# Block-diagonal products on 64-row tiles of TensorE, one transposed Y for the features' transform, and a Nyquist row in two parts

## The chip, the cores and the metric

The kernel runs on one core of one Trainium2 chip. The metric is the device time of one execution in microseconds (us), lower is better; the number given for a kernel is the median of its runs. A core has TensorE (PE, matrix products; its weight loads are listed as PEld), VectorE (DVE), ScalarE (ACT), GpSimd (POOL) and SyncE (SP), which here issues the DMAs. Products write into PSUM, which has eight banks of 512 f32 columns on 128 partitions; DVE and ACT read it.

## What is computed

Three layers, batch 8, sequence 576, width 512 (8 heads of 64):

```python
# 1. Nystroem attention, m = 32 landmarks, per batch and head
A = sm(q, k_lm); Bm = sm(q_lm, k_lm); C = sm(q_lm, k)      # softmaxes
Z = ...                                                     # six steps Z = 2 Z - Z Bm Z
x = A @ Z @ C @ v
# 2. Fourier mixing and a feed-forward layer
u = x + real(fft(fft(x, axis=seq), axis=feature))
un = (u - mean(u)) / sqrt(var(u) + 1e-6)
y = u + relu(un @ w_ch1) @ w_ch2
# 3. gated channel mixing with a token shift
out = sigmoid(xr @ w_r) * (relu(xk @ w_k) ** 2 @ w_v)
```

## The kernel before

**Stages.** The attention and the mixing (`phase1`) work per batch; layer 2 (`norm`, `block_a`) works on nine blocks of 512 tokens, layer 3 (`prep`, `Gated`) on the same nine blocks behind it. Block i needs the batches that cover its tokens, so block 0 needs batch 0, and block 1 batches 0 and 1. While `block_a(i)` runs its long stream of f16 products (tiles `ph`, banks 4 and 5, and `acc`, banks 0 to 3), the products of later batches and normalisations are put between them. They take their PSUM tile, `gp`, from the banks left, and those are two once the blocks run; `psum(2)` takes two at once. Three blocks of `u` (tiles `ub`) fit in SBUF.

**Order.** Nothing is ordered by hand. `Plan.record` writes down each operation with its engine, an estimated cost and what it depends on; `Plan.issue` (line 375) then simulates the engines and gives each engine a fixed order: of the operations that are ready, the one with the longest tail of work behind it plus its stage's lead goes first (line 141: block products 1000, the start 400, batches 200, conversions of weights 170). DMAs stand in SyncE's queue in the same way. Where the simulation leaves PE idle, it puts in filler products (`warm`, line 1037: tile `spare`, or zeros added into the open `acc`). The products of the blocks are chained in their written order. The estimate of a product (`mm`, line 322) is its columns, four times for f32, divided by 4 or 2 where its weights have at most 32 or 64 columns, as such products lie beside each other on column tiles of the array. In the profile an f32 product has two records and an f32 transpose one.

**Weights.** `w_ch1` and `w_ch2` come as 64-bit numbers and are converted on ACT and DVE piece by piece (`Weights.run`: tiles `wst`, `wtop`, `more`, into `w1h`, `w1l`, `w2h`, `w2l`) while batch 0 and block 0 run.

**A batch.** `chain_a` makes the scores A (three tiles `A0` to `A2` of 97 rows, line 663), folds them by the sequence's symmetry, multiplies them with cosines and sines over the sequence (tiles `acs`: AC and AS) and transposes them (tile `at`: AT). `chain_b` and `series` (line 806) give Y = Z C v per head, four heads to a group g of 128 partitions (32 landmarks of each head). Line 817 writes it out as block diagonal `bdY`: 256 columns per group, where head h's 32 rows hold its 64 features and the other rows hold zeros (`mask4`).

**The tail of a batch** (line 894) is what the diff is about:
- `bdY` is transposed in four pieces, of which only the blocks on the diagonal are copied to `YT`.
- The features' transform: four products of `YT` pieces (128 rows, 64 columns) with `cs` (128 x 512 each) give cosine and sine parts `YC`, `YS` and the Nyquist column `yn`; two products side by side on two column halves of the array.
- `mixed(j)` (line 927) multiplies YC with AC and YS with AS for the 128 frequencies of slot block j, and DVE (or POOL) forms difference and sum, d1 and d2, in one buffer each.
- `xu(t)` (line 947) does x = A Y for slot block t = 0 to 3: two products with a piece of `bdY` as 128 x 128 weights, of 289 and 288 columns; DVE adds d and writes `u`.
- The Nyquist row is two products of one column of weights over 289 columns, which ACT copies into row 0 of d1 and d2 between `xu(0)` and `xu(2)`.

**norm(i)** (line 1111) has two forms. For i < 2 the mean is four products with `ones` on the four tiles of u, and the sum of squares 32 records of products of one column (`one`). For later blocks DVE and POOL add the four tiles first, the mean is one product, POOL adds the squares, and `token_sums` transposes them in four pieces, which DVE reduces.

Of the kernel before, what the change touches and what calls it, by code (L numbers as in the profile page):

```python
# [37 lines left out]
def slot_features():  # L38
    f = np.arange(DM)
    f[257:] = 512 - np.arange(1, 256)  # L40
    return f
# [151 lines left out]
class Plan:  # L193
# [127 lines left out]

    def mm(self, out, lhsT, rhs, start, stop, chain=False, **kw):

        cost = wide(rhs) / 2400.0 + 0.0025
        if rhs.dtype == F32:
            cost = max(4 * cost, 0.17)
        share = 4 if wide(lhsT) <= 32 else 2 if wide(lhsT) <= 64 else 1

        def run():
            self.nc.tensor.matmul(  # L330
                out.real(), lhsT=lhsT.real(), rhs=rhs.real(), start=start, stop=stop, **kw
            )

        op = self.record("pe", run, cost / share, [out], [lhsT, rhs])
# [244 lines left out]
def phase1(a, iss, psum, const, pool, ident, ublock):  # L579
# [162 lines left out]
    def chain_b(b):  # L742
# [63 lines left out]
        def series():  # L806
# [21 lines left out]
            g_.tensor_copy(bdY[:, 1, 0:1], bdY[:, 1, 256:257])  # L828

# [64 lines left out]
    def tail(b):  # L894

        bdY = T["bdY", b]
        psT = psum()[0]
        for pr in range(4):
            g, hp = pr // 2, pr % 2
            tr(  # L900
                psT[:, 128 * pr:128 * pr + 128],
                bdY[:, g, g + 128 * hp:g + 128 * hp + 128], ident,
            )
        YT = tile([128, 2, 2, 64], "YT", "t1")
        pT = psT.rearrange("p (g x) -> p g x", g=2)
        s_.activation(YT[:, :, 0], pT[:, :, 0:64], AF.Copy)
        s_.activation(YT[:, :, 1], pT[:, :, 192:256], AF.Copy)
        YC, YS = [
# [4 lines left out]
        g_.memset(YS[:, :, 0:1], 0.0)  # L913
        for g in range(2):
            ps = psum()[0]
            for hp in range(2):
                mm(
                    ps[64 * hp:64 * hp + 64, :], YT[:, g, hp, :], cs[:, 2 * g + hp, :],
                    True, True,
                )  # L920
            s_.activation(YC[:, g], ps[:, 0:256], AF.Copy)
# [5 lines left out]
        def mixed(j):  # L927
            pc, pq = psum(2)
# [7 lines left out]
            s_.activation(cp, pc[:, 0:HS], AF.Copy)  # L936
            d1 = tile([128, HS], "d1")
            d2 = tile([128, HS], "d2")
            v_.tensor_tensor(d1, cp, pq[:, 0:HS], op=ALU.subtract)
# [3 lines left out]
            else:  # L943
                v_.tensor_tensor(d2, cp, pq[:, 0:HS], op=ALU.add)
            return d1, d2

        def xu(t, da, db):
            g = t // 2
            pa, pb = psum()[0], psum()[0]
            lt = bdY[:, g, 128 * (t % 2):128 * (t % 2) + 128]  # L950
            mm(pa[:, 0:HS], lt, AT[0][:, g], True, True)
            mm(pb[:, 0:288], lt, AT[1][:, g, 0:288], True, True)
            base = S * b
            for i, lo, hi in cuts(base, base + HS):
                v_.tensor_tensor(
                    ublock(i)[t][:, lo - BLK * i:hi - BLK * i],
                    pa[:, lo - base:hi - base], da[:, lo - base:hi - base], op=ALU.add,
                )
            end = base + S
            for i, lo, hi in cuts(base + HS, end):  # L960
                l, h = lo - BLK * i, hi - BLK * i
                v_.tensor_tensor(
                    ublock(i)[t][:, h - 1:(l - 1 if l else None):-1],
                    pb[:, end - hi + 1:end - lo + 1], db[:, end - hi + 1:end - lo + 1],
                    op=ALU.add,
                )
# [12 lines left out]

# [11 lines left out]
def build(nc, tc, a):  # L991
# [5 lines left out]
    with stack, tc.manual_schedule():  # L997
# [113 lines left out]
        def norm(i):  # L1111
# [15 lines left out]
            if i < 2:  # L1127
                ps = gp()[0]
# [274 lines left out]
def consts():  # L1403
    mask2 = np.zeros((128, 2), np.float32)
    mask4 = np.zeros((128, 4), np.float32)
    for p in range(128):
        mask2[p, p // 64] = 1.0 / 18
        mask4[p, p // 32] = 1.0
    eye32 = np.tile(np.eye(M, dtype=np.float32), (4, 1))
    bones = np.kron(np.eye(4), np.ones((M, M))).astype(np.float32)  # L1410
# [13 lines left out]
    kk = np.arange(257)  # L1424
    for i in range(4):
        for p in range(128):
            f = 128 * i + p if i < 2 else 511 - (128 * (i - 2) + p)
            ang = 2 * np.pi * ((f * kk) % DM) / DM
            cs[p, i, 0:257] = np.cos(ang)
            cs[p, i, 257:512] = np.sin(ang[1:256])  # L1430
    return dict(
        mask2=mask2, mask4=mask4, eye32=eye32, bones=bones,
        ident=np.eye(128, dtype=np.float32),
# [48 lines left out]
```

## Time and profile before

| | us |
|---|---|
| median of 3 runs | 1536.48 (1536.45 to 1540.12) |
| the profiled execution | 1536.68 |
| its span, from the first to the last instruction | 1534.9 |
| PE busy in the span | 1522.2 |
| DVE, ACT, POOL busy in the span | 818.0, 578.2, 287.2 |

The profile lists every instruction of one execution with start and duration. Groups of instructions are named as out<-in by the program's tiles, with rows*columns of the weights and rows x columns of the moving operand for a product. Products are pipelined, so a product's duration holds its latency; how long it holds the engine is read from one start to the next. The timeline merges like instructions that follow each other; its columns are start, time from the first start to the last end, engine, line, operation, tiles, shape and count, and in brackets idle time before. PEclk is the granted share of TensorE's clock.

### The profile page before, as it was taken

To read this page: it belongs to the slowest core of one execution; us is meant where nothing else is said; L and a number is where in the kernel's file an instruction comes from. 1 tells how busy PE (TensorE), PEld (TensorE's weight loads), DVE (VectorE), ACT (ScalarE), POOL (GpSimd) and SP (SyncE) were. 2 spreads that over 40 slices of the span, in tenths; PEclk is the share of its full clock that TensorE was granted. 3 is DMA by queue.
4 is the path that set the end of the run, shared out by engine and by line. 5 is a ranking of instruction groups with operands and counts; after the bars stand their busy time and mean duration, and the time that the engine had idled before them with its cause. 6 is when DMAs were issued, how large, how long until landed. Compare 5 with 4: busy or idle time off the path is not lost.

```text
span 1534.9 us, 20950 instructions
## 1 busy us (share of the span) xinstructions
PE 1522.2 (99%) x8284; PEld 777.8 (51%) x8284; DVE 818.0 (53%) x1698; ACT 578.2 (38%) x1181; POOL 287.2 (19%) x351
## 2 busy tenths in 40 slices
PE   9999999999999999999999999999999999999998
PEld 5655555555645645645544444444444444444443
DVE  7888667667636426426135171212777765653222
ACT  4667464445413213213212131113655544443221
POOL 3021103113102102102002040001544432231100
PEclk9999999999999999999999999999999999999999
DMA  8434252433301001000004000002011101000000
GB/s 290 159 125 153 79 179 73 144 122 123 101 35 63 32 28 62 2 28 1 1 28 165 1 28 1 28 0 83 28 56 55 55 28 55 28 13 16 28 28 28
DMA packets 43586, 97.86 MB, mean 64 GB/s; under 512 B 4064, under 2 KB 9440, under 8 KB 42976
## 3 DMA queue, kind: packets, MB, share of 16 engines
q1 hardware_dynamic: 43488, 96.53, 18.4%
q8 instruction: 65, 1.06, 0.3%
q14 instruction: 33, 0.27, 0.1%
HBM read 72.39 MB, written 24.12 MB: 63 GB/s over the span
## 4 chain that ended last, share of the span: by engine, by line
PE 96%; DMA 1%; DVE 1%; ACT 1%; issue 0%; SPq 0%; POOL 0%; ACTq 0%; DVEq 0%
PE ph L330 37%; PE acc L330 36%; PE gp L330 21%; PE gp L346 2%; DMA ident<-in_ident 1%; DMA wst<-in_w_ch 0%; DVE small L186 0%; PE spare L1043 0%; SPq L315 0%; DVE uc L186 0%; DMA out<-o 0%; DVE d L186 0%; ACT d L186 0%; ACT wtop L186 0%; DVE o L186 0%
## 5 line engine op out<-in xcount | busy, mean ns | idle before, releaser
L330 PE MATMUL ph<-un,w1h 128*128 128x512 f16 x1152 | 349.9, 379 | 0.4 <-DVE uc L186 0.3
L330 PE MATMUL acc<-h,w2h 128*128 128x512 f16 x1152 | 348.5, 379 | 0.0
L186 DVE SCALAR_TENSOR_TENSOR h<-ph,h 128x512 f16<-128x512 f32 x144 | 99.2, 689 | 302.6 <-ACT h L186 302.2
L186 ACT ACTIVATE h<-ph 128x512 f16<-128x512 f32 x144 | 85.9, 596 | 390.7 <-PE ph L330 390.4
L330 PE MATMUL ph<-un,w1l 128*128 128x512 f16 x576 | 218.6, 380 | 0.0
L330 PE MATMUL acc<-h,w2l 128*128 128x512 f16 x576 | 218.3, 379 | 0.1
L330 PE MATMUL ph<-xk,w_k 128*128 128x512 f16 x864 | 199.6, 379 | 0.0
L330 PE MATMUL acc<-w_v,k 128*128 128x512 f16 x864 | 198.9, 379 | 0.0
L330 PEld LDWEIGHTS <-w2h 128*128 128x128 f16 x1152 | 113.0, 99 | 128.4 <-issue 5.7
L330 PEld LDWEIGHTS <-w1h 128*128 128x128 f16 x1152 | 112.7, 99 | 127.8 <-issue 7.4
L330 PEld LDWEIGHTS <-k 128*128 128x128 f16 x864 | 84.5, 98 | 100.6
L330 PEld LDWEIGHTS <-w_k 128*128 128x128 f16 x864 | 84.5, 98 | 99.7
L186 DVE TENSOR_TENSOR rk<-rk 128x512 f32<-128x512 f32 x72 | 55.5, 770 | 146.3 <-ACT rk L186 145.9
L330 PE MATMUL gp<-w_r,xr 128*128 128x512 f16 x432 | 99.3, 379 | 0.7 <-ACT rs L186 0.7
L186 ACT ACTIVATE rk<-ph 128x512 f32<-128x512 f32 x72 | 42.9, 596 | 129.2 <-PE ph L330 121.6
L330 PEld LDWEIGHTS <-w1l 128*128 128x128 f16 x576 | 57.1, 99 | 65.1 <-issue 4.4
L330 PEld LDWEIGHTS <-w2l 128*128 128x128 f16 x576 | 56.7, 98 | 63.2 <-issue 0.6
L186 DVE TENSOR_TENSOR k<-rk,k 128x512 f16<-128x512 f32 x72 | 59.3, 823 | 29.2 <-ACT k L186 29.0
L186 POOL TENSOR_TENSOR sq<-sq 128x513 f32<-128x513 f32 x27 | 36.7, 1360 | 198.6 <-ACT sq L186 198.1
L186 POOL TENSOR_TENSOR xr<-xt,xr 128x512 f16<-128x512 f32 x36 | 48.6, 1374 | 112.1 <-ACT xr L186 112.0
L330 PEld LDWEIGHTS <-xr 128*128 128x128 f16 x432 | 42.3, 98 | 51.4 <-issue 0.9
L186 DVE TENSOR_TENSOR xt<-xt,rs 128x512 f32<-128x512 f32 x72 | 60.5, 869 | 2.9 <-ACT rs L186 2.8
(162 smaller groups left out, 1919.1 us busy)
## 6 DMA issues: line engine op xcount, KB each, us to landing
wst<-in_w_ch SPq DMA_DIRECT2D x24, 512.0 KB, 3.9
q<-in_q SPq DMA_DIRECT2D x16, 578.0 KB, 5.1
k<-in_k SPq DMA_DIRECT2D x16, 576.0 KB, 4.9
ys<-ub SPq DMA_DIRECT2D x36, 256.0 KB, 2.1
out<-o SPq DMA_DIRECT2D x36, 256.0 KB, 2.1
yb<-ys SPq DMA_DIRECT2D x8, 1026.0 KB, 5.1
v<-in_v SPq DMA_DIRECT2D x8, 1024.0 KB, 5.9
more<-in_w_ch SPq DMA_DIRECT2D x8, 512.0 KB, 4.6
```

Source lines behind the costliest of these rows:

```text
L186: f(real(out), *map(real, args), **{k: real(x) for k, x in kw.items()})
L330: self.nc.tensor.matmul(out.real(), lhsT=lhsT.real(), rhs=rhs.real(), start=start, stop=stop, **kw)
L346: self.nc.tensor.transpose(out.real(), in_.real(), ident.real())
```

## The change

Per batch, on the same numbers:
- `bdY` gets two heads' columns instead of four (`maskp` in place of `mask4`): rows 0 to 63 and rows 64 to 127 now hold two heads each, in the same 128 columns. A dense `Y` is kept beside it.
- One transpose of `Y` (both groups beside each other) replaces the four of `bdY`. `cs` is laid out anew, so that each head is one product with 64 rows and 32 columns of weights; the eight of them stand on eight tiles of the array and write two banks.
- `xu(g)` does both slot blocks of a group: pairs of products, on rows 0 to 63 and rows 64 to 127, into two banks taken together; first the two of 289 columns, then the two of 288.
- Both `mixed` come first, with four tiles d1 to d4; d3 and d4 lie in the slots of A0 and A1.
- The Nyquist row is split at column 145 into two parts on two column tiles; ACT copies it in four pieces, and two rows are copied from d3 and d4 to d1 and d2, as the slots of two features change places.
- The planner's cost of a product is divided by 2 where two row tiles lie beside each other (`beside`).
- `norm(1)` takes the form of the later blocks.

```diff
 def slot_features():
     f = np.arange(DM)
-    f[257:] = 512 - np.arange(1, 256)
+    f[257:384] = 512 - np.arange(1, 128)
+    f[385:] = 384 - np.arange(1, 128)
+    f[256], f[384] = 384, 256
...
-        op = self.record("pe", run, cost / share, [out], [lhsT, rhs])
+        op = self.record("pe", run, cost / share / beside, [out], [lhsT, rhs])
...
+    maskp = load_const("maskp", [128, 2])
...
-        A = [tile([97, 2, 256], f"A{c}") for c in range(3)]
+        A = [
+            tile([128, 512], f"A{c}")[0:97].rearrange("p (x m) -> p x m", x=2) for c in range(3)
+        ]
...
-            bdY = T["bdY", b] = tile([128, 2, 260], "bdY")
+            bdY = T["bdY", b] = tile([128, 2, 130], "bdY")
+            Y = T["Y", b] = tile([128, 2, D], "Y")
...
+                s_.activation(Y[:, g], psY[:, D * g:D * g + D], AF.Copy, scale=rc[:, g:g + 1])
                 v_.scalar_tensor_tensor(
-                    bdY[:, g, g:g + 256].rearrange("p (h d) -> p h d", d=D),
-                    psY[:, D * g:D * g + D].unsqueeze(1).to_broadcast([128, 4, D]),
-                    rc[:, g:g + 1], mask4.unsqueeze(2).to_broadcast([128, 4, D]),
+                    bdY[:, g, g:g + 128].rearrange("p (h d) -> p h d", d=D),
+                    psY[:, D * g:D * g + D].unsqueeze(1).to_broadcast([128, 2, D]),
+                    rc[:, g:g + 1], maskp.unsqueeze(2).to_broadcast([128, 2, D]),
...
-        for pr in range(4):
-            g, hp = pr // 2, pr % 2
-            tr(
-                psT[:, 128 * pr:128 * pr + 128],
-                bdY[:, g, g + 128 * hp:g + 128 * hp + 128], ident,
-            )
-        YT = tile([128, 2, 2, 64], "YT", "t1")
...
+        tr(psT[:, 0:128], T["Y", b].rearrange("p g d -> p (g d)"), ident)
+        YT = tile([128, 2, 128], "YT", "t1")[:, 0]
+        s_.activation(YT, psT[:, 0:128], AF.Copy)
...
-        for g in range(2):
-            ps = psum()[0]
-            for hp in range(2):
+        ps2 = psum(2)
+        for h in range(4):
+            for g in range(2):
+                r = slice(64 * g, 64 * g + 64)
                 mm(
-                    ps[64 * hp:64 * hp + 64, :], YT[:, g, hp, :], cs[:, 2 * g + hp, :],
-                    True, True,
+                    ps2[g][M * h:M * h + M, :], YT[r, M * h:M * h + M], cs[r, h, :],
+                    True, True, beside=2, tile_position=(64 * g, M * h),
                 )
...
+        def xu(g, ds):
+
+            rows = [slice(64 * x, 64 * x + 64) for x in range(2)]
             base = S * b
+            end = base + S
+            pa = psum(2)
+            for x, r in enumerate(rows):
+                mm(pa[x][:, 0:HS], bdY[r, g, 0:128], AT[0][r, g], True, True, beside=2)
+            for x in range(2):
+                for i, lo, hi in cuts(base, base + HS):
+                    v_.tensor_tensor(
+                        ublock(i)[2 * g + x][:, lo - BLK * i:hi - BLK * i],
+                        pa[x][:, lo - base:hi - base], ds[x][0][:, lo - base:hi - base],
+                        op=ALU.add,
+                    )
+            pb = psum(2)
+            for x, r in enumerate(rows):
+                mm(pb[x][:, 0:288], bdY[r, g, 0:128], AT[1][r, g, 0:288], True, True, beside=2)
...
+        d1, d2 = tile([128, HS], "d1"), tile([128, HS], "d2")
+        d3, d4 = [tile([128, 512], n, t)[:, 0:HS] for n, t in (("d3", "A0"), ("d4", "A1"))]
+        mixed(0, d1, d2)
+        mixed(1, d3, d4)
+        xu(0, ((d1, d2), (d3, d4)))
+
+        s_.activation(d1[0:1, :], d3[0:1, :], AF.Copy)
+        s_.activation(d2[0:1, :], d4[0:1, :], AF.Copy)
+        psN = psum()[0]
+        parts = (0, 0, 145), (32, 145, HS)
+        for g in range(2):
+            for p, lo, hi in parts:
+                mm(
+                    psN[p:p + 1, lo:hi], yn[:, g:g + 1], AC[:, g, lo:hi], g == 0, g == 1,
+                    tile_position=(0, p),
                 )
...
-        d1, d2 = mixed(0)
-        xu(0, d1, d2)
-        psN = psum()[0]
-        for g in range(2):
-            mm(psN[0:1, 0:HS], yn[:, g:g + 1], AC[:, g], g == 0, g == 1)
-        s_.activation(d1[0:1, :], psN[0:1, 0:HS], AF.Copy)
-        s_.activation(d2[0:1, :], psN[0:1, 0:HS], AF.Copy)
-        xu(2, d2, d1)
-        d1, d2 = mixed(1)
-        xu(1, d1, d2)
-        xu(3, d2, d1)
+        for d in (d3, d4):
+            for p, lo, hi in parts:
+                s_.activation(d[0:1, lo:hi], psN[p:p + 1, lo:hi], AF.Copy)
+        xu(1, ((d2, d1), (d4, d3)))
...
-            if i < 2:
+            if i < 1:
```

The last edit stands twice, at lines 1116 and 1127.

## Rows read from the trace of the kernel before

**Rows 1.** The page, parts 1 and 4: busy time and the chain of waits.
```profile
PE 1522.2 (99%) x8284; PEld 777.8 (51%) x8284; DVE 818.0 (53%) x1698; ACT 578.2 (38%) x1181; POOL 287.2 (19%) x351
...
PE 96%; DMA 1%; DVE 1%; ACT 1%; issue 0%; SPq 0%; POOL 0%; ACTq 0%; DVEq 0%
```

**Rows 2.** Stretches start:end, length; busy us and count by engine; clock; DMA.
```profile
5.00:70.00 65.00, 62.49 (x472) 40.96 (x469) 55.10 (x139) 35.18 (x91) 12.50 (x17) 1.00 0.67 235
77.00:207.00 130.00, 129.27 (x833) 71.37 (x833) 100.91 (x236) 79.95 (x164) 23.80 (x30) 0.99 0.38 124
340.00:455.00 115.00, 115.00 (x688) 62.75 (x687) 67.61 (x161) 44.62 (x101) 17.51 (x21) 1.00 0.29 95
```
In rows 2 the engines stand in the order PE, PEld, DVE, ACT, POOL.

**Rows 3.** Groups of PE by tiles and shape, fillers: busy, mean ns, idle before.
```profile
L1043 PE MATMUL spare<-zero 128*128 128x512 f16 x89 | 24.5, 415 | 2.3 <-POOL zero L186 2.3
...
L1043 PE MATMUL acc<-zero 128*128 128x512 f16 x13 | 3.5, 380 | 0.0
```

**Rows 4.** Timeline of PE, batch 7: transposes and the features' transform.
```profile
737.43 0.60 PE L346 MATMUL gp<-ident,bdY 128*128 128x128 f32 x4
737.87 0.41 PE L346 MATMUL gp<-ident,A 96*128 96x96 f32 x3
...
738.55 0.38 PE L330 MATMUL acc<-h,w2h 128*128 128x512 f16 x1
738.86 1.95 PE L330 MATMUL gp<-c_cs,YT 128*64 128x512 f32 x8
740.74 0.39 PE L330 MATMUL acc<-h,w2h 128*128 128x512 f16 x1
```

**Rows 5.** Timeline of PE, batch 6: Nyquist row and a product with bdY.
```profile
689.30 0.59 PE L330 MATMUL ph<-un,w1h 128*128 128x512 f16 x2
689.83 1.14 PE L330 MATMUL gp<-acs,yn 128*1 128x289 f32 x4
690.89 0.39 PE L330 MATMUL ph<-un,w1l 128*128 128x512 f16 x1
691.12 0.65 PE L330 MATMUL gp<-at,bdY 128*128 128x289 f32 x2
691.61 0.59 PE L330 MATMUL acc<-h,w2h 128*128 128x512 f16 x2
```

**Rows 6.** Timeline of PE, normalisation of block 1: mean, then squares.
```profile
169.10 3.64 PE L330 MATMUL gp<-ub,one 128*128 128x512 f32 x8
172.58 0.38 PE L330 MATMUL acc<-h,w2l 128*128 128x512 f16 x1
...
175.39 3.63 PE L330 MATMUL gp<-one,tmp 128*128 128x1 f32 x32
178.88 0.61 PE L330 MATMUL ph<-un,w1h 128*128 128x512 f16 x2
```

**Rows 7.** The stretch behind it, in the columns of rows 2.
```profile
179.00:183.00 4.00, 4.00 (x16) 1.26 (x14) 3.32 (x15) 0.00 (x0) 0.91 (x2) 0.57 0.00 0
```

**Rows 8.** Timeline of PE at the start: batch 0's tail, block 0's mean and first product.
```profile
43.02 1.30 PE L330 MATMUL gp<-acs,Ae 128*128 128x289 f32 x4 [0.86 <-ACT Ae L186]
...
49.72 1.16 PE L330 MATMUL gp<-kbd,q 128*97 128x64 f32 x12
50.71 1.20 PE L330 MATMUL gp<-acs,Ae 128*128 128x289 f32 x4
...
61.09 3.67 PE L330 MATMUL gp<-ub,one 128*128 128x512 f32 x8
...
77.34 0.89 PE L330 MATMUL ph<-un,w1h 128*128 128x512 f16 x2 [0.26 <-DVE uc L186]
```

**Rows 9.** Timeline of SyncE's queue: the issue of a small constant.
```profile
6.69 0.33 SPq L315 DMA_DIRECT2D c_eye<-in_eye  x1
```

**Rows 10.** Timeline of DVE: the low half of the last piece of w_ch2.
```profile
202.65 0.68 DVE L186 SCALAR_TENSOR_TENSOR w2l<-wst,w2h 128x512 f16<-128x512 f32 x1
```

**Rows 11.** Timeline of PE: block 0's last products with that piece.
```profile
204.12 0.60 PE L330 MATMUL acc<-h,w2h 128*128 128x512 f16 x2
```

More of the change, by code (lines that the diff above doesn't have):

```diff
@@ L320, in load, with mm @@
         )
-    def mm(self, out, lhsT, rhs, start, stop, chain=False, **kw):
+    def mm(self, out, lhsT, rhs, start, stop, chain=False, beside=1, **kw):
         cost = wide(rhs) / 2400.0 + 0.0025
@@ L821, in series @@
             for g in range(2):
+                s_.activation(Y[:, g], psY[:, D * g:D * g + D], AF.Copy, scale=rc[:, g:g + 1])
                 v_.scalar_tensor_tensor(
-                    bdY[:, g, g:g + 256].rearrange("p (h d) -> p h d", d=D),
-                    psY[:, D * g:D * g + D].unsqueeze(1).to_broadcast([128, 4, D]),
-                    rc[:, g:g + 1], mask4.unsqueeze(2).to_broadcast([128, 4, D]),
+                    bdY[:, g, g:g + 128].rearrange("p (h d) -> p h d", d=D),
+                    psY[:, D * g:D * g + D].unsqueeze(1).to_broadcast([128, 2, D]),
+                    rc[:, g:g + 1], maskp.unsqueeze(2).to_broadcast([128, 2, D]),
                     op0=ALU.mult, op1=ALU.mult,
                 )
-            g_.tensor_copy(bdY[:, 1, 0:1], bdY[:, 1, 256:257])
+            g_.tensor_copy(bdY[:, 1, 0:1], bdY[:, 1, 128:129])
         return series
@@ L897, in tail @@
         psT = psum()[0]
-        for pr in range(4):
-            g, hp = pr // 2, pr % 2
-            tr(
-                psT[:, 128 * pr:128 * pr + 128],
-                bdY[:, g, g + 128 * hp:g + 128 * hp + 128], ident,
-            )
-        YT = tile([128, 2, 2, 64], "YT", "t1")
-        pT = psT.rearrange("p (g x) -> p g x", g=2)
-        s_.activation(YT[:, :, 0], pT[:, :, 0:64], AF.Copy)
-        s_.activation(YT[:, :, 1], pT[:, :, 192:256], AF.Copy)
+        tr(psT[:, 0:128], T["Y", b].rearrange("p g d -> p (g d)"), ident)
+        YT = tile([128, 2, 128], "YT", "t1")[:, 0]
+        s_.activation(YT, psT[:, 0:128], AF.Copy)
         YC, YS = [
@@ L913, in tail @@
         g_.memset(YS[:, :, 0:1], 0.0)
-        for g in range(2):
-            ps = psum()[0]
-            for hp in range(2):
-                mm(
-                    ps[64 * hp:64 * hp + 64, :], YT[:, g, hp, :], cs[:, 2 * g + hp, :],
-                    True, True,
+        ps2 = psum(2)
+        for h in range(4):
+            for g in range(2):
+                r = slice(64 * g, 64 * g + 64)
+                mm(
+                    ps2[g][M * h:M * h + M, :], YT[r, M * h:M * h + M], cs[r, h, :],
+                    True, True, beside=2, tile_position=(64 * g, M * h),
                 )
+        for g, ps in enumerate(ps2):
             s_.activation(YC[:, g], ps[:, 0:256], AF.Copy)
@@ L925, in tail, with mixed @@
         AT = T["at", b]
-        def mixed(j):
+        def mixed(j, d1, d2):
             pc, pq = psum(2)
@@ L936, in mixed @@
             s_.activation(cp, pc[:, 0:HS], AF.Copy)
-            d1 = tile([128, HS], "d1")
-            d2 = tile([128, HS], "d2")
             v_.tensor_tensor(d1, cp, pq[:, 0:HS], op=ALU.subtract)
@@ L944, in mixed @@
                 v_.tensor_tensor(d2, cp, pq[:, 0:HS], op=ALU.add)
[L945 to L952, printed above, removed]
-            base = S * b
[L954 to L957, printed above, removed]
-                )
[L959 to L966, printed above, removed]
@@ L968, in tail @@
-        d1, d2 = mixed(0)
-        xu(0, d1, d2)
-        psN = psum()[0]
-        for g in range(2):
-            mm(psN[0:1, 0:HS], yn[:, g:g + 1], AC[:, g], g == 0, g == 1)
-        s_.activation(d1[0:1, :], psN[0:1, 0:HS], AF.Copy)
-        s_.activation(d2[0:1, :], psN[0:1, 0:HS], AF.Copy)
-        xu(2, d2, d1)
-        d1, d2 = mixed(1)
-        xu(1, d1, d2)
-        xu(3, d2, d1)
+        def xu(g, ds):
+            rows = [slice(64 * x, 64 * x + 64) for x in range(2)]
+            base = S * b
+            end = base + S
[12 more added lines that the diff above has]
+                mm(pb[x][:, 0:288], bdY[r, g, 0:128], AT[1][r, g, 0:288], True, True, beside=2)
+            for x in range(2):
+                for i, lo, hi in cuts(base + HS, end):
+                    l, h = lo - BLK * i, hi - BLK * i
+                    v_.tensor_tensor(
+                        ublock(i)[2 * g + x][:, h - 1:(l - 1 if l else None):-1],
+                        pb[x][:, end - hi + 1:end - lo + 1],
+                        ds[x][1][:, end - hi + 1:end - lo + 1], op=ALU.add,
+                    )
@@ L1126, in norm @@
             r, t1, var = small(), small(), small()
-            if i < 2:
+            if i < 1:
                 ps = gp()[0]
@@ L1405, in consts @@
     mask4 = np.zeros((128, 4), np.float32)
+    maskp = np.zeros((128, 2), np.float32)
     for p in range(128):
@@ L1408, in consts @@
         mask4[p, p // 32] = 1.0
+        maskp[p, p // 32 % 2] = 1.0
     eye32 = np.tile(np.eye(M, dtype=np.float32), (4, 1))
@@ L1424, in consts @@
     kk = np.arange(257)
-    for i in range(4):
+    for h in range(4):
         for p in range(128):
-            f = 128 * i + p if i < 2 else 511 - (128 * (i - 2) + p)
+            f = D * h + p if p < D else 511 - D * h - (p - D)
             ang = 2 * np.pi * ((f * kk) % DM) / DM
-            cs[p, i, 0:257] = np.cos(ang)
-            cs[p, i, 257:512] = np.sin(ang[1:256])
+            cs[p, h, 0:257] = np.cos(ang)
+            cs[p, h, 257:512] = np.sin(ang[1:256])
     return dict(
-        mask2=mask2, mask4=mask4, eye32=eye32, bones=bones,
+        mask2=mask2, mask4=mask4, maskp=maskp, eye32=eye32, bones=bones,
         ident=np.eye(128, dtype=np.float32),
```

## The prediction

> **What bounds the kernel now.** I read the page's busy times and its chain of waits first: TensorE (PE) is busy for nearly the whole span, and the chain that ended last is 96% PE [rows 1]. A busy PE can still be one that only fills time, so the second look is at the filler products, which the planner puts where it expects PE to idle. 89 of them go to a spare bank and 13 to an open accumulator [rows 3]; the 13 add zeros in the stretch of block 0, and behind it there are none. So I cut the run in three. **Start**, up to 77 us: PE waits for batch 0's chain and for the normalisation of block 0, and fills. **Front**, 77 to 207 us, block 0: PE is full, but DVE (VectorE) is busy for 101 of 130 us and ACT (ScalarE) for 80, because the weights are converted here [rows 2]. **Rest**, from 207 us on: PE is full with DVE at 68 and ACT at 45 of 115 us [rows 2]. In the rest a microsecond taken from PE is a microsecond of time. Batches 2 to 7 lie there; batch 1 and the normalisation of block 1 lie in the front, batch 0 in the start.
>
> **The change, part by part, per batch.** I read a product's cost from one start to the next, not from its duration, which holds the pipeline's latency.
>
> Transposes: four start in 0.44 us (737.43 to 737.87) [rows 4]. One stays at 0.11, so -0.33.
>
> Products with cs: after the f16 product at 738.55 (0.22 us each in that stream) they hold PE from 738.77 to 740.74, 1.97 us [rows 4]. A record of 512 f32 columns takes 0.435 (eight in 172.58 - 169.10) [rows 6], and four products are eight records. One after the other they would take 3.48; two column halves run beside each other, in 4 x 0.435 = 1.74. The other 0.23 is the price of going into the divided array and out again. Now eight products stand on eight tiles, two records each: 2 x 0.435 + 0.23 = 1.10, so -0.87.
>
> Nyquist row: behind two f16 products (0.43 us) from 689.30 it holds PE from 689.73 to 690.89, 1.16 us: four records of 0.245 and 0.19 for in and out [rows 5]. Two column tiles with half the columns take half, 0.49 + 0.19 = 0.68, so -0.48.
>
> Products with bdY: one of 289 columns takes 0.49 (691.12 to 691.61) [rows 5], and there are eight, 3.92. Now there are four pairs. With two free banks in the steady state, both taken by one pair, the next pair waits until DVE has emptied them, other products come between, and every pair pays for in and out. No row has a pair of 64-row halves. Its bounds are 0.49 (fully beside) and 0.98 (one after the other); the nearest row, the column halves with cs [rows 4], stands at fully beside, so I take 0.49. In and out cost 0.19 with one column of weights [rows 5] and 0.23 with 64 [rows 4]; these have 128, so I take 0.27, with ends at 0.19 and at 0.49, which would leave no gain. 4 x 0.76 = 3.04, so -0.88.
>
> That is 0.33 + 0.87 + 0.48 + 0.88 = 2.56 us per batch, and 15.4 us for batches 2 to 7.
>
> A rule speaks against these pairs. The rows with cs show two column halves starting as one [rows 4], which is only possible if the first record of the second product doesn't wait for the second record of the first. The Trainium skill, page "TensorE: Matmul & The Clock Gate", section "Part 3: Packing small matmuls — row/col tiling", says that matmuls start and end strictly in program order; by that, if the two records of a product follow each other in the program, a pair would take three records instead of two. What this would do to row halves is the third rival.
>
> Normalisation of block 1: the mean's eight records (3.48 us) become two (0.87), and the 32 one-column records (178.88 - 175.39 = 3.49) become four transposes (0.44) [rows 6]: -2.61 - 3.05 = -5.66. Behind those 32, the clock is granted at 0.57 over 4 us, so 3.4 us run at the lower of its two levels and 1.7 us are lost [rows 7]. I expect that stretch to vanish: -1.7. The new path adds three sums on DVE and POOL ahead of the mean and three on POOL behind it; block 1's first product has to wait for that, and it is late by some 3 us if the end of block 0 doesn't hide it.
>
> Added beside PE: two ACT copies of Y, four more ACT copies of Nyquist parts, one fewer of YT; two DVE products at half width. In the rest ACT idles over half the time [rows 2], so I cost these at nothing; uncovered they would be some 2 us per batch at 0.3 to 0.4 each. The second half of xu now waits for the last of six ACT copies instead of two, and the bank of the Nyquist row is held as long; the block's stream runs meanwhile. The maskp load is one more issue on SyncE's queue at the start, like that of c_eye, 0.33 us [rows 9]; constants behind it in the queue move by that, and batch 0 needs it late.
>
> Moved: both mixed() now come before the first xu, with d3 and d4 in the slots of A0 and A1. So the next batch's scores wait until xu is through. Twelve of these records take 1.0 us (49.72 to 50.71) [rows 8], the 48 of a batch some 4 us, which the front loses as filling for PE until batch 1 is done; in the rest they are only moved.
>
> **Start and front.** Batch 0's second mixed started 7.7 us after the first (43.02, 50.71), and the mean at 61.09 [rows 8]. A mixed is 2.1 us long, so up to 5.6 us are to be had; DVE is busy 55 of 65 us there [rows 2], so it may be 0. In the front 2.56 + 5.66 + 1.7 = 9.9 us leave PE. But its end is tied to the weights: the last low half is done at 203.33 and its stage's products begin at 204.12 [rows 10, 11]. If the conversions don't move, only 0.8 us come through; if they move along, 9.9 + 5.6 = 15.5. The conversions rank behind the batches on DVE and ACT, so they gain when those finish earlier, but DVE has little room; I take the middle, 8.
>
> Sum: 15.4 + 8 = 23.4 us. The profiled execution took 1536.68 us, 1.8 beyond its span and 0.2 over the median: 1513.3.
>
> **The rivals.**
> 1. *The front gives nothing*: weights, DVE and ACT set its end. For it: pieces come just ahead of their use [rows 10, 11]. Against: neither engine is full over the 130 us [rows 2]. 15.4 + 0.8 = 16.2, so 1520.5. The Trainium skill, page "TensorEngine Tiling (Array Packing)", section "PSUM Bottleneck", warns in this sense that tiling speeds up TensorE and not the emptying of PSUM; in the rest the trace speaks against it, with DVE at 68 of 115 us [rows 2]. Chance 0.17.
> 2. *The change doesn't do what it says*: two 64-row halves run one after the other. cs stays at four record times, no gain; a pair costs 0.98 + 0.27 instead of 0.98, four times +0.27. With -0.33 and -0.48 a batch loses 0.27 in all: +1.6 over six. The start and front keep about half of 7.4 less 0.3: 1534.7. For it: no row shows it otherwise. Against: column halves do run together [rows 4]. Chance 0.07.
> 3. *Slower: strict order of starts between row halves.* A product's second record occupies its tile until the first is through, and the next product starts only with it. The eight products with cs become a chain of nine records, 3.9 + 0.23 = 4.15 instead of 1.97; a pair is three records, 0.73 + 0.27 = 1.0. A batch then loses 2.18 + 0.08 - 0.81 = 1.45, six lose 8.7, and the front still wins some 3: 1542.4. It decides from the point where the losses in cs pass 0.8 us a batch. Against: the rows with cs, which by it would last 5 x 0.435 [rows 4]. Chance 0.05.
> 4. *Everything comes through*: the front's 15.5 and in and out at 0.19, 32 x 0.08 = 2.6 more: 1503. Chance 0.08.
>
> **How the numbers follow.** My forecast has 0.63. The range goes from 1503.5 (rival 4) to 1525: only 0.8 from the front and in and out at 0.49 in the rest, 24 x 0.22 = 5.3 more than forecast, give 1525.8. It leaves out rivals 2 and 3 and the fringe. A measurement of this kernel can tell 0.3%, 4.6 us, from no change. Forecast, rivals 1 and 4 and a little of 2 are faster, 0.89; most of 2 is the same, 0.06; rival 3 is slower, 0.05.
>
> **What would show it.** In the profile after: cs as 16 records within 1.1 us; at,bdY as pairs, records starting a few ns apart in two banks, some 0.76 us from the product before to the one behind; one transpose of Y per batch; no drop of the clock near 180 us; block 1 starting near 199 instead of 207; DVE and ACT busy times nearly the same. I am wrong in size if pairs take 1.0 us or over, and in mechanism if fillers or waits appear behind block 1, or block 1 waits for its normalisation.

## The result and the profile after

The changed kernel took 1519.67 us (median of 4 runs, 1518.84 to 1519.99). The kernel before, run beside it on the same chip, took 1537.92, so the ratio is 0.9879, 95% interval 0.9862 to 0.9896. The forecast was 1513.3 with a range of 1503.5 to 1525: the time lies in the range. The forecast took 23.4 us off the profiled execution. Between the spans of the two profiles 16.8 came, and between the two medians above 18.3.

Busy time and chain of waits on the page after, as in [rows 1]:

```profile
PE 1504.3 (99%) x8358; PEld 756.7 (50%) x8358; DVE 814.8 (54%) x1700; ACT 591.3 (39%) x1221; POOL 291.3 (19%) x355
...
PE 97%; DVE 1%; ACT 1%; issue 0%; DMA 0%; POOL 0%; DVEq 0%; POOLq 0%
```

PE is 17.9 us less busy, and still the chain. The stretches of the kernel after, in the columns of [rows 2] (the first is the start, then block 0's front; the last two are the stretch behind the first normalisation and the one that [rows 7] showed):

```profile
5.00:70.00 65.00, 64.44 (x496) 41.70 (x494) 53.41 (x147) 34.30 (x88) 12.44 (x17) 0.95 0.64 229
79.00:197.00 118.00, 117.44 (x711) 62.08 (x709) 87.72 (x200) 74.37 (x148) 22.04 (x26) 1.00 0.39 125
...
60.90:67.70 6.80, 6.80 (x26) 2.99 (x26) 5.55 (x23) 1.69 (x4) 0.00 (x0) 0.50 0.66 228
...
179.00:183.00 4.00, 4.00 (x32) 2.70 (x31) 3.10 (x13) 2.30 (x4) 0.05 (x1) 1.00 0.30 62
```

The low clock at 179 is gone. Another, at the start, now lasts 6.8 us; before it lasted 3.4, at 70.1. The front takes 118 us instead of 130. The fillers of the kernel after, as in [rows 3]:

```profile
L1058 PE MATMUL spare<-zero 128*128 128x512 f16 x112 | 31.5, 431 | 2.3 <-POOL zero L188 2.3
...
L1058 PE MATMUL acc<-zero 128*128 128x512 f16 x26 | 6.7, 381 | 0.0
```

There are 23 more at the start and 13 more in the front: TensorE now has time there that nothing uses. To see where the 16.8 us between the two spans (1534.9 and 1518.0) came from, I cut both profiles at the first product of block 0 and of block 1:

| | block 0 starts | block 1 starts | rest, to the end |
|---|---|---|---|
| before | 77.3 | 207.1 | 1327.7 |
| after | 79.0 | 197.1 | 1320.9 |
| difference | +1.7 | -10.0 | -6.8 |

The cut isn't clean, because the planner orders the work anew. The products with v and ET of a batch are 80. These two rows, one from each kernel, are the instructions with the tile `ET` up to block 1's start. Busy time and count stand for PE first, then for PEld and ACT:

```profile
0.00:207.10 207.10, 5.69 (x240) 4.06 (x240) 4.26 (x9) 0.98 0.48 161
```

```profile
0.00:197.10 197.10, 4.46 (x160) 2.94 (x160) 2.69 (x6) 0.98 0.48 162
```

Before, three batches' products lay ahead of block 1's start, now two. With the products of k with qbd, the transposes of E and c_cosT products that moved with them, some 5 us of batch 2's work went from the front to the rest (from one start to the next: 1.7 for v with ET, 1.1 for k with qbd, 1.1 for E, 1.1 for c_cosT). Without this move the rest would be shorter by some 12 us and block 1 would start some 5 us earlier than before, not 10.

**The products themselves** came out as worked out. Timeline of PE after: the mean and the squares of block 1's normalisation, batch 6's one transpose of Y, its products with cs, a pair of xu, and the Nyquist row:

```profile
170.95 1.02 PE L333 MATMUL gp<-tmp,one 128*128 128x512 f32 x2
...
179.78 0.61 PE L349 MATMUL gp<-ident,tmp 128*128 128x128 f32 x4
...
620.55 0.27 PE L349 MATMUL gp<-ident,Y 128*128 128x128 f32 x1
...
624.29 0.38 PE L333 MATMUL ph<-un,w1h 128*128 128x512 f16 x1
624.60 1.09 PE L333 MATMUL gp<-c_cs,YT 64*32 64x512 f32 x16
625.62 0.39 PE L333 MATMUL ph<-un,w1h 128*128 128x512 f16 x1
...
669.20 0.38 PE L333 MATMUL ph<-un,w1l 128*128 128x512 f16 x1
669.50 0.76 PE L333 MATMUL gp<-at,bdY 64*128 64x288 f32 x4
670.19 0.61 PE L333 MATMUL ph<-un,w1h 128*128 128x512 f16 x2
...
676.82 0.38 PE L333 MATMUL acc<-h,w2h 128*128 128x512 f16 x1
677.13 0.66 PE L333 MATMUL gp<-acs,yn 128*1 128x145 f32 x8
677.72 0.39 PE L333 MATMUL acc<-h,w2h 128*128 128x512 f16 x1
```

An f16 product holds PE for 0.22 us, so cs holds it from 624.51 to 625.62, 1.11 us (forecast 1.10), a pair of xu from 669.42 to 670.19, 0.77 (forecast 0.76), the Nyquist row from 677.04 to 677.72, 0.68 (forecast 0.68).

**A wait that I had not seen** stands in the rest. Waits of PE after (us in total, times, the longest):

```profile
PE gp L333 <- DVE bdY L188: 2.2, 5, 0.5
...
PE gp L333 <- ACT Y L188: 0.4, 1, 0.4
```

It comes once a batch, at the products with c_sinT. Timeline of the kernel after, all engines, batch 5:

```profile
503.02 0.31 ACT L188 ACTIVATE Y<-gp,bst 128x64 f32<-128x64 f32 x1 [2.34 <-PE gp L333]
...
503.37 0.35 DVE L188 SCALAR_TENSOR_TENSOR bdY<-gp,bst,c_maskp 128x128 f32<-128x128 f32 x1 [1.23 <-ACT Y L188]
...
503.66 0.38 PE L333 MATMUL acc<-h,w2h 128*128 128x512 f16 x1
...
503.76 0.31 ACT L188 ACTIVATE Y<-gp,bst 128x64 f32<-128x64 f32 x1 [0.42 <-DVE bdY L188]
...
504.10 0.35 DVE L188 SCALAR_TENSOR_TENSOR bdY<-gp,bst,c_maskp 128x128 f32<-128x128 f32 x1 [0.38 <-ACT Y L188]
...
504.51 0.78 PE L333 MATMUL gp<-c_sinT,Ao 96*128 96x289 f16 x5 [0.47 <-DVE bdY L188]
```

The same step in the timeline of DVE before:

```profile
619.25 0.88 DVE L186 SCALAR_TENSOR_TENSOR bdY<-gp,bst,c_mask 128x256 f32<-128x256 f32 x2 [0.21 <-PE gp L330]
```

Before, DVE alone emptied the bank of Y in 0.88 us. Now ACT and DVE read it by turns, each waiting for the other (the brackets), 503.02 to 504.45, 1.43 us. These waits are for semaphores that the program sets; whether both engines could read the bank at once, no run shows. From the product before (503.66 + 0.22 = 503.88) PE stands for 0.63 us. The six of these waits take 0.57 to 0.63 us each from one start to the next, 3.6 in all.

**The start** gave nothing, although the mean of block 0 runs 10.6 us earlier (50.47, was 61.09 in [rows 8]). Timeline of PE after:

```profile
50.47 3.65 PE L333 MATMUL gp<-ub,one 128*128 128x512 f32 x8
...
57.54 3.99 PE L333 MATMUL gp<-one,tmp 128*128 128x1 f32 x32
...
62.49 5.96 PE L1058 MATMUL spare<-zero 128*128 128x512 f16 x15
68.29 0.60 PE L349 MATMUL gp<-ident,small 128*128 128x128 f32 x4
...
77.53 1.62 PE L349 MATMUL gp<-ident,E 128*128 128x128 f32 x9 [0.16 <-ACT E L188]
78.99 0.59 PE L333 MATMUL ph<-un,w1h 128*128 128x512 f16 x2
```

The operands of block 0 are ready by 73.8, with the last of them on DVE:

```profile
72.53 1.29 DVE L188 TENSOR_TENSOR un<-uc,un 128x512 f16<-128x512 f32 x2
```

Yet the first product comes at 78.99, behind batch 1's transposes of E. Ahead of that the 15 fillers of 62.49 take 5.80 us at the clock of 0.50, where as many take 3.3 at full clock. Behind them stands `ident,small`, a step of block 0's normalisation, whose operand DVE had done at 64.2.

And **the end of the front** is again tied to the last low half. Timelines of DVE and PE after:

```profile
193.58 0.68 DVE L188 SCALAR_TENSOR_TENSOR w2l<-wst,w2h 128x512 f16<-128x512 f32 x1
```

```profile
194.96 0.39 PE L333 MATMUL acc<-h,w2l 128*128 128x512 f16 x1
...
197.13 0.59 PE L333 MATMUL ph<-un,w1h 128*128 128x512 f16 x2
```

It is done at 194.26 (203.33 in [rows 10]); its first product comes at 194.96, and block 1 starts at 197.13, 2.9 us after it was done.

### The profile page after: what moved, and what is told of

It is laid out like the page before. It is cut to its first block, busy times and chain, and to the rows that moved or that the text cites. A ratio compares the mean times of both kernels' runs of the same rounds, so it can differ in the third digit from the quotient of the medians.

```text
span 1518.0 us, 21130 instructions
## 1 busy us (share of the span) xinstructions
PE 1504.3 (99%) x8358; PEld 756.7 (50%) x8358; DVE 814.8 (54%) x1700; ACT 591.3 (39%) x1221; POOL 291.3 (19%) x355
## 4 chain that ended last, share of the span: by engine, by line
PE 97%; DVE 1%; ACT 1%; issue 0%; DMA 0%; POOL 0%; DVEq 0%; POOLq 0%
PE ph L333 37%; PE acc L333 37%; PE gp L333 20%; PE gp L349 2%; PE spare L1058 1%; DVE small L188 0%; DVE bdY L188 0%; PE acc L1058 0%; ACT Y L188 0%; DVE uc L188 0%; ACT E L188 0%; ACT un L188 0%; DMA out<-o 0%; DVE cst L188 0%; DVE o L188 0%
## 5 line engine op out<-in xcount | busy, mean ns | idle before, releaser
L333 PEld LDWEIGHTS <-w2h 128*128 128x128 f16 x1152 | 112.3, 98 | 129.0 <-issue 9.1
```

The costliest lines, as they stand in the source:

```text
L333: self.nc.tensor.matmul(out.real(), lhsT=lhsT.real(), rhs=rhs.real(), start=start, stop=stop, **kw)
```

## The experiments

Two questions were open. **What sets the end of the front after the change?** Theory A: PE, and the start was lost to a bank of PSUM, since block 0's first product wants a bank that holds batch 1's scores. Theory B: the conversion of the weights, whatever PE does. **Do row halves run side by side, and what does the wait for Y cost?** All runs, with the cuts of the table above taken from each run's profile (us; each ratio is to the kernel before as it ran beside that run; "fillers" are those into the accumulator; "block" is one block's length in the rest, from block 3's start to block 4's):

| run | time | ratio to before | block 0 starts | block 1 starts | rest | block | fillers |
|---|---|---|---|---|---|---|---|
| before | 1537.92 | | 77.3 | 207.1 | 1327.7 | 115.1 | 13 |
| after | 1519.67 | 0.9879 [0.9862, 0.9896] | 79.0 | 197.1 | 1320.9 | 112.9 | 26 |
| e1 | 1523.85 | 0.9916 [0.9899, 0.9932] | 74.0 | 200.9 | 1320.2 | 112.9 | 31 |
| e2 | 1523.73 | 0.9914 [0.9899, 0.9928] | 77.9 | 202.3 | 1319.3 | 112.9 | 13 |
| e3 | 1533.98 | 0.9981 [0.9971, 0.9990] | 77.7 | 204.2 | 1328.0 | 115.1 | 26 |
| e4 | 1513.53 | 0.9846 [0.9832, 0.9861] | 77.8 | 190.0 | 1321.0 | 112.9 | 4 |
| e5 | 1529.79 | 0.9954 [0.9939, 0.9969] | 79.0 | 196.5 | 1330.7 | 115.1 | 12 |
| e6 | 1524.72 | 0.9920 [0.9905, 0.9935] | 79.3 | 205.8 | 1317.2 | 113.6 | 21 |
| e7 | 1545.04 | 1.0052 [1.0035, 1.0069] | 72.9 | 230.2 | 1314.4 | 114.8 | 0 |
| e8 | 1520.46 | 0.9892 [0.9877, 0.9907] | 72.1 | 199.8 | 1318.6 | 112.3 | 20 |
| e9 | 1518.38 | 0.9874 [0.9857, 0.9890] | 71.1 | 196.1 | 1319.9 | 112.3 | 0 |
| e10 | 1513.25 | 0.9835 [0.9820, 0.9850] | 73.2 | 194.2 | 1317.5 | 112.3 | 20 |
| e11 | 1538.63 | 1.0002 [0.9992, 1.0011] | 77.5 | 205.7 | 1327.9 | 115.1 | 13 |
| e12 | 1519.02 | 0.9876 [0.9859, 0.9894] | 73.5 | 195.7 | 1320.3 | 113.0 | 17 |

Each edit is to the kernel after, except in e3, e7 and e11, which edit the kernel before.

### e1: banks 4 and 5 kept for block 0

```diff
-        fixed, holds = {WARM}, {}
+        fixed, holds = {WARM, 4, 5}, {}
```

> The changed kernel, with banks 4 and 5 kept for the blocks' products from the start on (gp tiles of batches 0 and 1 get five banks instead of seven). In the changed kernel block 0's operands are there at 71 to 74 us, and its first product comes at 79.0, behind the transposes of E of batch 1. Theory A (the start was lost to that wait for a PSUM bank, and PE is the bound behind it): first product near 72 to 73, the block's end near 191, time 1513 to 1515. Theory B (block 0's end is set by the conversion of the weights): first product as early, but the end of block 0 stays near 197 and the time within 2 us of 1519.7, with more fillers in the stretch of block 0.

1523.85 us. The bank was what held block 0's start: it comes at 74.0 instead of 79.0. But block 0 ends 3.7 us later than in the kernel after, at 200.9. That is neither A's 191 nor B's 197. The front is 8.7 us longer. PE stands idle in it for 5.0 us (0.6 after), and 2.1 us are batch 1's transposes of E and products of k with qbd, which lay ahead of block 0 after; five more fillers are 1.5. The edit takes two banks from the batches, so it doesn't tell what an earlier start would give by itself, and it doesn't decide between A and B.

### e2: block 1's normalisation as before

The edit stands twice, here and in e3.

```diff
-            if i < 1:
+            if i < 2:
...
```

> The changed kernel with norm(1) in the form that it had before (mean of four products, 32 one-column records). By the terms of my sum it costs PE 5.7 us and 1.7 us of slow clock. Theory A (PE bounds block 0): time up by 6 to 7.5, to 1526 to 1527. Theory B (the weights bound block 0's end): the stretch's 26 fillers take it up, and time rises by 0 to 3, to 1520 to 1522.

1523.73 us, 4.1 more than after, between the two expectations. The 7.4 us (5.66 of products, 1.7 of clock) that PE has more to do are paid about half by the fillers, which fall from 26 to 13 (3.4 us), and half by the time. So the fillers are slack that work can take, as B has it; but 13 of them stay while the time rises, which neither theory gives alone. Block 1 starts 5.2 later, and 2.2 of that is batch 2's work, which lay in the rest after.

### e3: block 1's normalisation alone, in the kernel before

```diff
-            if i < 2:
+            if i < 1:
...
```

> The kernel before with the edit of norm(1) alone. Theory A: down by 6 to 7.5, to 1529 to 1530. Theory B: 13 more or so fillers in the stretch of block 0, time down by 0 to 3, 1534 to 1537. The drop of the clock near 180 us is gone by both.

1533.98 us, ratio 0.9981, a gain under the 0.3%. In the profile block 1 starts 2.9 us earlier and the fillers rise from 13 to 26. Of the 7.4 us that left PE, 13 fillers took 3.4 (13 x 0.26). The time is B's; as in e2, about half of PE's 7.4 us shows in it.

### e4: the conversions' lead at 230 instead of 170

The plan adds a stage's lead to the rank of its operations. At 230 the conversions go ahead of the batches behind batch 0, which have 200; this is what some expectations call "230 us ahead".

```diff
-NOW, START, CONVERT, SOON = 1000.0, 400.0, 170.0, 200.0
+NOW, START, CONVERT, SOON = 1000.0, 400.0, 230.0, 200.0
```

> The changed kernel with the lead of the weights' conversions at 230 instead of 170, so that on DVE, ACT and SyncE they go ahead of the batches behind batch 0 (200). Theory B: the pieces come earlier, the 26 fillers in the stretch of block 0 go, block 0 ends near 190 and the time falls by 5 to 8, to 1512 to 1515. Theory A: conversions weren't late, batch 1 and norm(1) get late instead, and the time stays or rises by 1 to 4.

1513.53 us, 6.1 less than after, and about the forecast of the whole change. The last low half in DVE's timeline:

```profile
185.34 0.69 DVE L188 SCALAR_TENSOR_TENSOR w2l<-wst,w2h 128x512 f16<-128x512 f32 x1
```

The last low half is done at 186.0 instead of 194.3, block 1 starts at 190.0, and 22 fillers are gone (22 x 0.26 = 5.7 us, by 6.7 us for 26), with the rest unchanged. In the kernel after, the conversions' place in the order held the end of the front: B.

### e5: the two halves of a pair one after the other

Both column parts of xu stay in the rows of one half before the other half comes, so no two products stand beside each other there. The sums are the same.

```diff
-            pa = psum(2)
             for x, r in enumerate(rows):
-                mm(pa[x][:, 0:HS], bdY[r, g, 0:128], AT[0][r, g], True, True, beside=2)
+                pa, pb = psum(2)
+                mm(pa[:, 0:HS], bdY[r, g, 0:128], AT[0][r, g], True, True)
+                mm(pb[:, 0:288], bdY[r, g, 0:128], AT[1][r, g, 0:288], True, True)
...
```

> The changed kernel, but xu takes the two products (289 and 288 columns) of one row half behind each other, then those of the other half; as many visits to the divided array, no two halves beside each other. If halves run beside each other in the changed kernel, a visit grows from 0.78 to about 1.26 us, 4 x 0.48 = 1.9 us per batch: blocks 3 and 4 take 115 us instead of 113, and behind block 1's start some 11.5 us more; time 1529 to 1532. If they didn't run beside each other, nothing changes.

A block is 115.1 us again and the rest 9.8 longer. A pair in PE's timeline:

```profile
675.68 0.38 PE L333 MATMUL ph<-un,w1l 128*128 128x512 f16 x1
675.99 1.24 PE L333 MATMUL gp<-at,bdY 64*128 64x289 f32 x4
677.16 0.60 PE L333 MATMUL ph<-un,w1h 128*128 128x512 f16 x2
```

From 675.90 to 677.16 are 1.26 us, against 0.77 with the halves side by side. So two 64-row halves do run beside each other when they follow each other in the program. Rivals 2 and 3 are ruled out.

### e6: xu on 128 rows, the rest of the change kept

bdY and xu are as in the kernel before, from one transposed Y; Y takes BB's slot.

```diff
...
-                mm(pa[x][:, 0:HS], bdY[r, g, 0:128], AT[0][r, g], True, True, beside=2)
+                mm(pa[x][:, 0:HS], bdY[:, g, x, 0:128], AT[0][:, g], True, True)
...
```

> The changed kernel with xu's products on 128 rows again (bdY per slot block with zeros in the other half's rows, two DVE products more), order and banks as in the changed kernel. By records a batch pays 8 x 0.49 = 3.92 us instead of 4 x 0.78 = 3.12: 0.8 per batch, some 5 us behind block 1's start, blocks 3 and 4 at 113.8; time 1523 to 1526 if the stretch of block 0 stays as it is. If going in and out of the divided array ate the gain, the blocks stay at 113.0.

A block is 113.6 us, 0.6 more than after (113.55 against 112.94; 113.8 was expected). Four pairs at 0.97 instead of 0.77 make 0.8 more; the wait at c_sinT is some 0.15 shorter here (0.48 from one start to the next). A pair here, in PE's timeline:

```profile
569.92 0.38 PE L333 MATMUL ph<-un,w1l 128*128 128x512 f16 x1
570.14 1.14 PE L333 MATMUL gp<-at,bdY 128*128 128x289 f32 x4
571.11 0.59 PE L333 MATMUL ph<-un,w1h 128*128 128x512 f16 x2
```

The total, 1524.72, doesn't price xu: block 1 starts at 205.8 and three batches' products with v and ET lie ahead of it again, so rest and front don't compare with those of the kernel after.

### e7: d1, d2 of the second mixed in the slots of A, in the kernel before

```diff
...
-            d1 = tile([128, HS], "d1")
-            d2 = tile([128, HS], "d2")
+            d1, d2 = [
+                tile([128, 512], n, t)[:, 0:HS] if j else tile([128, HS], n)
+                for n, t in (("d1", "A0"), ("d2", "A1"))
+            ]
```

> The kernel before with one part of the change: the second mixed's d1 and d2 in the slots of A0 and A1, so that it need not wait for the first xu, and the next batch's scores wait for the last. Theory B (weights set block 0's end): block 0's mean comes some 5 us earlier than 61.1, batch 2's scores come behind 160 instead of 126, and the time stays within 2 us of 1537. If the late scores cost the front, the time rises by 3 or more; if the earlier tail is worth something, it falls by 3 or more.

1545.04 us, 8.7 more than before: the expectation of "within 2" missed, and the second case, a rise of 3 or more if late scores cost the front, came. The second mixed no longer waits for the first xu and block 0 starts 4.4 us earlier, but its front takes 157.3 instead of 129.8. Part of that is moved work (the rest is 13.3 shorter). Most of the remainder is PE waiting, 10.6 us in that front (0.5 before), and running slowly; these two views show the longest of each, PE's waits and the stretch from 82 us:

```profile
PE ph L330 <- DVE A L186: 5.3, 1, 5.3
```

```profile
82.00:96.00 14.00, 7.28 (x97) 5.20 (x96) 12.76 (x36) 8.61 (x18) 2.23 (x3) 0.51 0.83 292
```

With the batch's tail drawn ahead, block 0 starts and then waits until DVE has emptied a bank of scores into A, and the scores now come behind xu. Whether the move of the slots costs the changed kernel as much can't be said; there no run has it by itself.

### e8: Y on DVE

```diff
-                s_.activation(Y[:, g], psY[:, D * g:D * g + D], AF.Copy, scale=rc[:, g:g + 1])
+                v_.tensor_scalar(
+                    Y[:, g], psY[:, D * g:D * g + D], rc[:, g:g + 1], None, op0=ALU.mult
+                )
```

> The changed kernel with the two copies of Y out of PSUM on DVE instead of ACT. In the changed kernel PE waits once a batch, some 0.6 us, for the first product with the sine table; its bank was held by psY, whose two readers ACT and DVE took turns: 1.43 us against 0.88 before. Theory C (two engines can't read the bank side by side, and the planner thinks they can): the waits go, six of them behind block 1's start, time down by 3 to 4.5, to 1515 to 1517. Theory D (two free banks are simply too few): the waits stay, time within 1 us of 1519.7.

The wait at c_sinT is gone. DVE makes the four reads of the bank in 0.99 us (505.27 to 506.26), against 1.43 by turns. Timelines of DVE and PE at the same step:

```profile
505.27 0.48 DVE L188 TENSOR_SCALAR Y<-gp,bst 128x64 f32<-128x64 f32 x2 [0.88 <-PE gp L333]
505.66 0.60 DVE L188 SCALAR_TENSOR_TENSOR bdY<-gp,bst,c_maskp 128x128 f32<-128x128 f32 x2
...
506.55 1.65 PE L333 MATMUL gp<-c_sinT,Ao 96*128 96x289 f16 x12
```

A block is 112.3, 0.6 less. The rest is 2.3 less and not 3.6; a new wait, for `ub` at 351, takes 0.9 us there from one start to the next. The front gave it back: block 1 starts 2.7 later, although block 0 starts 6.9 earlier. PE waits 3.9 us for BB, a tile of batch 1 that ACT copies out, and has the clock of 0.50 for 10.2 us:

```profile
79.00:89.20 10.20, 7.53 (x94) 4.71 (x95) 9.81 (x29) 7.70 (x16) 4.41 (x4) 0.50 0.45 150
```

The last low half is late too, done at 197.6 (194.3 after), with 20 fillers in the front. Which of the two set block 1's start, this run doesn't show.

### e9, e10, e12: the single gains together

e9 is e4's edit and e8's; e10 is e9 with e1's; e12 is e4's with e1's.

> The changed kernel with both single gains: the conversions planned 230 us ahead of their use (alone it gave 1513.5 and block 1 at 190.0) and the copies of Y on DVE (alone it took the waits at c_sinT away and gave the stretch behind block 1's start 2.3 us, 1320.9 to 1318.6). If DVE's extra work costs the front nothing once the conversions are early, both add: block 1 near 190, the rest near 1318.7, 1511 us. If the front gives it back as it did with Y alone (front 9.6 us longer, start 6.9 shorter), block 1 starts at 192 to 194 and the time is 1513 to 1516.

> The run before with banks 4 and 5 kept for block 0's first two products as well. If the conversions still set block 0's end, the earlier start of block 0 (74 instead of 79, as in the first run with these banks) comes to nothing or costs some us by a worse order: 1511 to 1518, with more fillers into the accumulator than the run before. If conversions that are early have freed TensorE to set the end, 3 to 5 us less than the run before and no such fillers.

> The changed kernel with the conversions 230 us ahead and banks 4 and 5 kept for block 0's first two products, Y back on ACT. With early conversions alone block 0 ran from 77.8 to 190.0 with 4 fillers into the accumulator left, so TensorE was nearly full. If TensorE now sets block 0's end, a start some 4 us earlier comes through: block 1 near 186.5, 1510 us, hardly more than those 4 fillers. If the conversions still set it, block 1 stays at 189 to 191 or comes later, 1513 to 1517, with 15 or more fillers into the accumulator.

e9: 1518.38 us, outside both expectations. No fillers are left in the front, yet block 1 starts at 196.1, not 190: PE waits, has the low clock, and waits again for block 1's normalisation (`un`). The wait for BB, the stretch behind it, and block 1's first product in PE's timeline:

```profile
PE gp L333 <- ACT BB L188: 4.6, 1, 4.6
```

```profile
80.50:90.70 10.20, 9.34 (x99) 5.28 (x100) 8.01 (x26) 5.89 (x11) 5.35 (x4) 0.50 0.63 190
```

```profile
196.05 0.38 PE L333 MATMUL ph<-un,w1h 128*128 128x512 f16 x1 [2.04 <-ACT un L188]
```

That is 4.6 us of waiting, 4.7 of 9.34 busy us lost to the clock, and 2.0 for the normalisation: the sign that the prediction named, hidden in the kernel after. e10: 1513.25 us, the fastest median, not to be told from e4, within the first case of its expectation. BB is waited for by only 0.2 us, but 20 fillers are back. e12: 1519.02 us, 5.5 more than e4 alone: block 0 starts 4.4 earlier and block 1 5.7 later. The front has 17 fillers, PE stands idle in it for 4.1 us (none in e4), and the last low half is done at 193.2 instead of 186.0:

```profile
192.33 0.82 DVE L188 SCALAR_TENSOR_TENSOR w2l<-wst,w2h 128x512 f16<-128x512 f32 x1
```

So beside e4's edit, too, keeping the banks for an earlier start of block 0 is worth nothing: it gives another order, with waits of the batches and later conversions. Beside e4's and e8's it is worth 5.1 us (e9 to e10), with the wait for BB gone. And the lead that gave 6.1 us in the kernel after gave 4.8 with the banks kept (e1 to e12) and 2.1, less than a measurement can tell, with Y on DVE (e8 to e9).

### e11: e4's edit in the kernel before

> The kernel before with one number changed: the conversions planned 230 us ahead instead of 170. It tells whether the 6 us that this number gave the changed kernel needed the change. If they were to be had in any case (conversions set block 0's end in both kernels), the gain is the same 6 us, 1531, with block 1 near 201. If the kernel before was held by TensorE in its front and had only its 13 fillers into the accumulator (13 x 0.275 = 3.6 us) to give, the gain is 0 to 3.6 us, 1533 to 1537, and those fillers go; the change is then what made room on TensorE that the conversions kept.

1538.63 us, ratio 1.0002: nothing. Fillers and the last low half:

```profile
L1043 PE MATMUL acc<-zero 128*128 128x512 f16 x13 | 3.5, 380 | 0.0
```

```profile
201.18 0.68 DVE L186 SCALAR_TENSOR_TENSOR w2l<-wst,w2h 128x512 f16<-128x512 f32 x1
```

The 13 fillers stay, and the last low half moves by 1.5 us. So e4's 6 us belong to the changed kernel: the change took work from PE in the front, the conversions as planned kept that time from being used, and only then is their lead worth something. Why the 13 fillers of the kernel before stay wasn't tried.

## Why the prediction was right or wrong

The direction, the range and the likeliest case were right. The 23.4 us were 6.6 too many by the spans, in two about equal parts.

- **Products in the rest: right.** Transposes, cs, the Nyquist row and a pair of xu cost within 0.01 us of their forecast. Taking "fully beside" from the column halves was right for row halves too, shown by e5, and so was 0.27 for in and out. The Trainium skill's page "TensorE: Matmul & The Clock Gate", section "Part 3: Packing small matmuls — row/col tiling", has matmuls start and end strictly in program order. Had that kept the second product of a pair behind both records of the first, as in rival 3, a pair would have taken 1.0 us; the 0.77 speaks against this reading.
- **"I cost these at nothing": wrong.** This was the step of the ACT copies of Y. That ACT idles over half the time said nothing about the bank that the copy shares with DVE. The two alternate, the bank comes free 0.55 us later, and the next product into it was already waiting. Six such waits make 3.6 us by starts; e8 shows it, with a block 0.6 shorter. The prediction named "waits behind block 1" as what would prove it wrong. The section "PSUM Bottleneck" of the Trainium skill's page "TensorEngine Tiling (Array Packing)", which I had set aside for the rest, advises to use ScalarE and VectorE both for emptying PSUM. On one bank that did not help here: 1.43 us by turns, 0.99 with DVE alone (e8).
- **Rest in sum**: -15.4 forecast; -6.8 by the cut, some -12 without the work moved into it, and the waits of 3.6 make the remainder. That this closes is partly luck: without its wait a block is 2.8 us shorter (115.1 to 112.3 in e8) where 2.56 were worked out, and where the other 0.2 come from wasn't looked into.
- **Normalisation of block 1: right in size on PE.** 7.36 us of forecast left PE and the drop of the clock at 180 went with them. But in the time about half of it was lost, by e2 and e3. The lateness of block 1 by its own normalisation was hidden, and shows only in e9.
- **"I take the middle, 8" for start and front: mis-sized.** It measured some 5: the start lost 1.7 and block 1's start came 10.0 earlier, of which some 5 were moved work. The error was to let room on PE and the conversions share the gain by halves, when rows gave a test: [rows 10, 11] show the last low half done just ahead of its products. Rival 1 had the mechanism, and e4 shows it for the kernel after: the conversions' lead alone was worth 6.1 us. Its figure, 0.8, was too low, because the conversions did move along some way, from 203.3 to 194.3.
- **The earlier mean of the start: no gain.** The bound of 0 was right. The cause was not DVE, but a bank (e1). What an earlier start would give by itself stays open: with the bank kept (e1, e12), and in e8 and e9 without it, block 0 started 5 to 8 us earlier and its front then held 4 to 9 us of PE's waits.
- **d3 and d4 in the slots of A**: costed as a loss of filling in the front. In the kernel before the move costs 8.7 us (e7); what part of this the changed kernel pays is open.

## What to carry to other kernels

When an engine is relieved in a stretch that a feeder follows closely, ask the feeder first: move it ahead in the same change (here one number of a planner gave 6.1 us, gave 4.8 and 2.1 beside two other small edits, and gave nothing without the change). When a second engine is to read a PSUM bank, price the bank and not the engine: look up who waits for it to come free. And where a planner makes the order, price a change by stretches with a constant amount of work (here one block in the rest, 115.1, 112.9 and 112.3 us); totals mixed three causes.

## What the hardware showed that was not expected

- Products of two 64-row halves in two banks run side by side: 0.77 us for two of 288 columns in float32, the way in and out with it, against 0.97 for the two on 128 rows and 1.26 one half after the other. More than half of what standing side by side saves (0.28 of 0.49 us) goes for in and out, so the gain over 128 rows is 0.2 us a pair.
- The clock at the start is as much a term as a wait. In the changed kernel it was granted at 0.50, the 1.2 GHz level, over 6.8 us behind the 32 one-column products (57.54), and there fillers that were meant to bridge the time held up the products behind them. In e8 and e9 PE waited 3.9 and 4.6 us for BB and had the low level for 10.2 us from the end of that wait on (in e8 from 1.9 us before it); in e9 that cost as much again as the wait (4.7 us).
